# Numerators of two q tiles in one go, and exponentials taken after the transposition

## The chip, the cores and the metric

The kernel runs on one core of a Trainium2 chip. The metric is device time in microseconds (us) of that core. Engines are named as the profile names them: PE (TensorE matmuls) and PEld (its weight loads), DVE (VectorE), ACT (ScalarE), POOL (GpSimd), SP (the queue that issues most DMAs).

## What is computed

The program chains three blocks on 2304 tokens: attention with random features, a two-layer block with softplus, and a gated block. The change touches the attention alone, and in it only the side of the queries. Cut to that:

```
def phi(x):                                   # x is q or k, scaled
    h = einsum('bhsd,md->bhsm', x, omega) - sum(x*x)/2
    h = h - max(h, axis=-1)
    return exp(h) / sqrt(m)
kv  = einsum('bhsm,bhsd->bhmd', k_p, v);  z = sum(k_p, axis=2)
num = einsum('bhsm,bhmd->bhsd', q_p, kv)
den = einsum('bhsm,bhm->bhs', q_p, z) + 1e-06
x   = num / den                               # B=4, H=8, S=576, D=64, m=128
```

For queries a factor that is the same for all 128 features falls out of num/den, so the kernel needs only exp(projection - its maximum).

## The kernel before

The 2304 tokens are cut into 18 q tiles of 128 tokens; each tile has two units of four heads (unit u belongs to tile u // 2, its second unit is odd). A loop over t = 0 to 21, here called turns, works on several tiles at once. Four kinds of PE work stand in a turn, and the text calls them by letters:

- **T** (`q_turn`, L390): eight transpositions of `qp` of tile t-2, two units of four heads; ACT then copies each unit out of PSUM to `qpt` (L392).
- **P** (`q_feat`, `project`, L93 on `qt`): twelve matmuls that project tile t. DVE takes the maximum over the features of each head, negated (`nmax`, L332), and ACT takes the exponential with that maximum as its bias, one instruction of 128x128 for each head (`features`, L337). `QLAG` holds the exponentials of one unit back by one.
- **N** (`q_num`, L93 on `kv,qpt`): numerators and denominators of tile t-3 (`NLAG`), sixteen matmuls of 64 columns for a unit's tile pair (32 instructions in the trace). DVE then adds 1e-6 (`den`, L407), takes the reciprocal (L408) and scales (`xt`, L411, 128x256 a unit).
- **X** (`x_turn`, L420): four transpositions of `xt` of tile t-4 (`XLAG`); ACT copies them to `xs`, and SP writes them to HBM.

So `xt` of a tile is made one turn before its X. Between these stand other steps: `split_q` casts a later q tile on DVE (L285) and subtracts on POOL (L286); `step` pumps a queue of jobs: at first the widening of weights (`Job`, L135 to L188: 128x1024 instructions on ACT and DVE), and from turn 10 on the operands of the next block (`operands`, L445 and L455, 128x768, read back from HBM). In turns 18 to 20 `fill` puts the first matmuls of the next block between. PSUM has eight banks in one pool (`ps`), which all of T, P, N and X share. A scheduler orders each engine's instructions from this program and sets the waits; every engine runs its own list strictly in that order.

Of the kernel before, what the change touches and what calls it, by code (L numbers as in the profile page):

```python
# [19 lines left out]
F32 = mybir.dt.float32  # L20
# [3 lines left out]
AF = mybir.ActivationFunctionType  # L24
ALU = mybir.AluOpType
# [3 lines left out]
M = 128  # L29
# [6 lines left out]
PSUM = bass.MemoryType.PSUM  # L36
DRAM = bass.MemoryType.DRAM
TLAG = 2
NLAG = 3
XLAG = 4  # L40
HALF = 64
PRE = 1
# [2 lines left out]
QLAG = 1  # L45
# [17 lines left out]
FILL = [18, 19, 20]  # L63
URGENT = 300
LINE = 32


@with_exitstack
def body(ctx: ExitStack, tc: tile.TileContext, q, k, k_rest, v, v_rest, om_t, w_in, w_out, w12, w3, wo, out):
    nc = tc.nc  # L70
    cp = ctx.enter_context(tc.tile_pool(name="cp", bufs=1))
    sm = ctx.enter_context(tc.tile_pool(name="sm", bufs=1))
    M_ = ctx.enter_context(tc.tile_pool(name="M_", bufs=14))
# [6 lines left out]
    def ps():  # L80
        return ps_.tile([128, 512], F32, tag="ps", name="ps")
# [156 lines left out]
    def step(rate):  # L238
        due[0] += rate
        while due[0] > 0:  # L240
            if not pump_one():
                due[0] = min(due[0], 2.0)
                break
            due[0] -= 1
# [25 lines left out]
    def pair(name, bufs):  # L270
        n = small.get(name, (None, 1))[1]
        if n:
            small[name] = sm.tile([128, 2, 4], F32, tag=name, bufs=bufs, name=name), 0
        else:
            small[name] = small[name][0], 1
        return small[name][0][:, 1 - bool(n)]
# [4 lines left out]
    def lined(pool, n, **kw):  # L281
        return pool.tile([128, -(-n // LINE) * LINE], F32, **kw)[:, :n]

# [25 lines left out]
    def load_q(t):  # L309
        if t < NT // 128:  # L310
            raw[t] = Q_.tile([128, 512], F32, tag="rawq", bufs=4, name="rawq")
            nc.sync.dma_start(out=raw[t], in_=q[t])

    def split_q(t):
        if t < NT // 128:
            if len(qbuf) < QBUF:
                qbuf.append(Q_.tile([128, 2, 512], FR, name=f"qt{len(qbuf)}"))
            qt = qbuf[t % QBUF]
            split(qt[:, 0, :], qt[:, 1, :], raw[t])
            qts[t] = qt.rearrange("p x (c t) -> p x c t", c=4)  # L320

    def project(lhs):
        pj = ps()
        for p in range(2):
            a = lhs(p)
            if len(a) == 2:
                mm3(pj[:, 256 * p:256 * p + 256], *a, *om_s, True, True)
            else:
                matmul(pj[:, 256 * p:256 * p + 256], *a, om, True, True)
        pj = pj.rearrange("p (h m) -> p h m", h=4)  # L330
        nmax = pair("nmax", 4)
        nc.vector.tensor_reduce(out=nmax, in_=pj, axis=AX.X, op=ALU.max, negate=True)  # L332
        return pj, nmax

    def features(pj, nmax, dst):
        for h in range(4):
            nc.scalar.activation(out=dst[:, h, :], in_=pj[:, h, :], func=AF.Exp, bias=nmax[:, h:h + 1])  # L337

    waiting = []

    def flush(n):
        while len(waiting) > n:
            waiting.pop(0)()
# [14 lines left out]
    def matmul_half(o, a, b, start, stop):  # L358
        for c in range(0, a.shape[-1], HALF):
            matmul(o[c:c + HALF], a[:, c:c + HALF], b, start, stop, skip_group_check=True)  # L360

    def kv_sum(i):
        b, g = divmod(i, 2)
        if g == 0:
            kvs[b] = lined(Q_, H * (D + 1), name=f"kv{b}").rearrange("p (h d) -> p h d", h=H)
        acc = ps()[:, 0:4 * (D + 1)].rearrange("p (h d) -> p h d", h=4)
        for h in range(4):
            for t in range(KT):
                matmul_half(acc[:, h, :], kps[i][:, t, h, :], vt[i][:, t, h, :], h == 0 and t == 0, False)
            r = 2 * (b // 2) + g  # L370
            matmul_half(acc[:, h, :], kpr[r][:, h, :], vrest[:, b % 2, r, h, :], False, h == 3)
        nc.scalar.copy(out=kvs[b][:, 4 * g:4 * g + 4, :], in_=acc)

    qp, qpt, xt = {}, {}, {}

    def q_feat(u):
        t, g = divmod(u, 2)
        p = project(lambda p: [qts[t][:, x, 2 * g + p, :] for x in range(2)])

        def exps():  # L380
            qp[u] = M_.tile([128, 4, M], F32, tag="m", name="qp")
            features(*p, qp[u])

        waiting.append(exps)
        flush(QLAG)

    def q_turn(u):
        tp = ps()
        for h in range(4):
            nc.tensor.transpose(tp[:, 128 * h:128 * h + 128], qp[u][:, h, :], ident)  # L390
        qpt[u] = M_.tile([128, 4, 128], F32, tag="m", name="qpt")
        nc.scalar.copy(out=qpt[u], in_=tp.rearrange("p (h t) -> p h t", h=4))  # L392

    def q_num(u):
        t, g = divmod(u, 2)
        nm = ps()
        nm = nm[:, 0:4 * (D + 1)].rearrange("p (h d) -> p h d", h=4)
        lo, hi = 128 * t, 128 * t + 128
        for h in range(4):
            a = lo  # L400
            while a < hi:
                b = a // S
                e = min(hi, (b + 1) * S)
                matmul_half(nm[a - lo:e - lo, h, :], qpt[u][:, h, a - lo:e - lo], kvs[b][:, 4 * g + h, :], True, True)
                a = e
        den = pair("den", 3)[:, :, None]
        nc.vector.tensor_scalar(out=den, in0=nm[:, :, D:D + 1], scalar1=1e-6 * M, scalar2=None, op0=ALU.add)  # L407
        nc.vector.reciprocal(out=den, in_=den)  # L408
        if g == 0:
            xt[t] = M_.tile([128, H, D], F32, tag="m", name="xt")  # L410
        nc.vector.tensor_tensor(  # L411
            out=xt[t][:, 4 * g:4 * g + 4, :], in0=nm[:, :, 0:D],
            in1=den.to_broadcast([128, 4, D]), op=ALU.mult,
        )

    def x_turn(t):
        tp = ps()
        x = xt[t].rearrange("p h d -> p (h d)")
        for c in range(KD):
            nc.tensor.transpose(tp[:, 128 * c:128 * c + 128], x[:, 128 * c:128 * c + 128], ident)  # L420
        xs = Q_.tile([128, KD, 128], F32, tag="xs", bufs=2, name="xs")
        nc.scalar.copy(out=xs, in_=tp.rearrange("p (c t) -> p c t", c=KD))
        nc.sync.dma_start(out=xd[:, :, 128 * t:128 * t + 128], in_=xs)
# [287 lines left out]
    nt = NT // 128  # L711
    begun = None

    def fill():
        nonlocal begun
        if begun is None:
            until(lambda: 0 in ready and win[0].done)
            x = Up1(0, 0, UP_RATES["Up1"][0])
            begun = x, x.begin_parts()
        next(begun[1], None)  # L720

    for t in range(nt + XLAG):
        for g in range(2):
            if 0 <= t - TLAG < nt:
                q_turn(2 * (t - TLAG) + g)
        for g in range(2):
            if t < nt:
                q_feat(2 * t + g)
            else:
                flush(0)  # L730
            step(JOB_Q[0 in xo])
        if t < nt:
            split_q(t + 2)
            load_q(t + 4)
        if t == 1:
            kv_sum(2 * B - 1)
            kstack.close()
            pools["X0"] = ctx.enter_context(tc.tile_pool(name="X0", bufs=28, side="right", reuse_waits="tile"))
        if 0 <= t - NLAG < nt:
            for g in range(2):  # L740
                q_num(2 * (t - NLAG) + g)
        if t >= XLAG:
            x_turn(t - XLAG)
            for c in range(2):
                if t - XLAG == 2 * N // 128 * (c + 1) - 1:
                    xo[c], ops = operands(c, xd, "X0")
                    queue += ops
        if t in FILL:
            fill()
# [426 lines left out]
```

## Time and profile before

| | us |
|---|---|
| median of 3 runs (815.7 to 816.96) | 816.19 |
| the profiled execution | 816.59 |
| its span, first to last instruction | 814.8 |
| PE busy, share of the span | 804.7 (99%) |
| DVE busy | 594.1 (73%) |
| ACT busy | 443.2 (54%) |
| granted TensorE clock, mean | 0.999 |

The turns with q tiles fill the stretch from about 53 to 137 us of the span; what comes before are the keys, what comes behind are the two dense blocks. A busy share over the whole span hides that stretch: there DVE and ACT are nearly full at times, and PE is the engine with gaps. Times in the rows below are from the start of the span. Where a row merges several instructions ("x8"), its time is that from the start of the first to the end of the last; two instructions of an engine overlap by some 0.08 us, so the distance from start to start is what an instruction takes of its engine.

### The profile page before, as it was taken

To read this page: it belongs to the slowest core of one execution; us is meant where nothing else is said; L and a number is where in the kernel's file an instruction comes from. 1 tells how busy PE (TensorE), PEld (TensorE's weight loads), DVE (VectorE), ACT (ScalarE), POOL (GpSimd) and SP (SyncE) were. 2 spreads that over 40 slices of the span, in tenths; PEclk is the share of its full clock that TensorE was granted. 3 is DMA by queue.
4 is the path that set the end of the run, shared out by engine and by line. 5 is a ranking of instruction groups with operands and counts; after the bars stand their busy time and mean duration, and the time that the engine had idled before them with its cause. 6 is when DMAs were issued, how large, how long until landed. Compare 5 with 4: busy or idle time off the path is not lost.

```text
span 814.8 us, 14545 instructions
## 1 busy us (share of the span) xinstructions
PE 804.7 (99%) x5520; PEld 755.6 (93%) x5520; DVE 594.1 (73%) x1005; ACT 443.2 (54%) x863; POOL 43.7 (5%) x38
## 2 busy tenths in 40 slices
PE   7999999999999999999999999999999999999998
PEld 6998989999999998888888889999999998889998
DVE  4888799878756666754569633898888866888861
ACT  6899998557545665755456422422334223674330
POOL 4623310000000000000000000000000000000000
PEclk9999999999999999999999999999999999999999
DMA  8733535756545457778984632455466556353212
GB/s 283 279 133 89 186 86 164 243 183 225 199 158 192 165 203 243 233 247 303 331 297 152 220 97 83 159 208 176 165 229 217 188 173 233 119 166 124 73 65 77
DMA packets 75717, 150.04 MB, mean 184 GB/s; under 512 B 7168, under 2 KB 44672, under 8 KB 75648
## 3 DMA queue, kind: packets, MB, share of 16 engines
q1 hardware_dynamic: 64560, 101.94, 37.6%
q10 hardware_dynamic: 11088, 47.18, 16.9%
q8 instruction: 43, 0.70, 0.4%
q14 instruction: 26, 0.21, 0.1%
HBM read 98.24 MB, written 50.86 MB: 183 GB/s over the span
## 4 chain that ended last, share of the span: by engine, by line
PE 85%; DVE 5%; ACT 4%; DMA 3%; issue 1%; SPq 0%; DVEq 0%; ACTq 0%
PE ps L93 84%; ACT kp L337 2%; DMA xq<-xd 1%; PE ps L390 1%; DVE s L445 1%; DMA raw<-in_w_in 1%; PE ps L420 1%; DVE nmax L332 1%; DVE xt L411 1%; ACT qp L337 1%; DVE qt L285 0%; DVE c L500 0%; DMA xd<-xs 0%; ACT f L135 0%; ACT raw L136 0%
## 5 line engine op out<-in xcount | busy, mean ns | idle before, releaser
L93 PE MATMUL ps<-dhi,lo 128*128 128x512 f32 (+1 forms) x320 | 117.7, 368 | 0.0
L93 PE MATMUL ps<-dlo,hi 128*128 128x512 f32 (+1 forms) x320 | 117.7, 368 | 0.0
L93 PE MATMUL ps<-dhi,hi 128*128 128x512 f32 (+1 forms) x320 | 117.5, 368 | 0.0
L621 DVE TENSOR_TENSOR dlo<-dn,dhi 128x512 fp32r<-128x512 f32 (+1 forms) x80 | 50.5, 635 | 48.4 <-ACT dhi L620 26.7
L620 ACT CAST dhi<-dn 128x512 fp32r<-128x512 f32 (+1 forms) x80 | 45.6, 576 | 56.9 <-DVE dlo L621 30.3
L500 DVE TENSOR_TENSOR c<-ps,u 128x384 f32<-128x384 f32 x144 | 71.4, 548 | 0.8
L93 PEld LDWEIGHTS ps<-dlo,hi 128*128 128x128 f32 x320 | 60.3, 189 | 10.1
L93 PEld LDWEIGHTS ps<-dhi,lo 128*128 128x128 f32 x320 | 60.3, 189 | 10.1
L93 PEld LDWEIGHTS ps<-dhi,hi 128*128 128x128 f32 x320 | 60.3, 189 | 9.8
L500 DVE TENSOR_TENSOR u<-ps,p 128x384 f32<-128x384 f32 x48 | 26.7, 555 | 58.0 <-PE ps L93 52.5
L135 ACT ACTIVATE f<-raw,bias 128x1024 f32<-128x1024 int16 (+2 forms) x43 | 46.6, 1090 | 33.5 <-DVE lo L176 8.5
L540 ACT ACTIVATE c<-c 128x384 f32<-128x384 f32 x72 | 35.0, 524 | 47.5 <-DVE c L500 47.5
L332 DVE TENSOR_REDUCE nmax<-ps 128x4 f32<-128x512 f32 x72 | 47.6, 680 | 17.8 <-PE ps L93 12.3
L139 DVE SCALAR_TENSOR_TENSOR f<-raw,f 128x1024 int32<-128x1024 f32 (+2 forms) x43 | 45.8, 1066 | 17.8 <-ACT raw L136 17.5
L507 ACT COPY p<-ps 128x384 f32<-128x384 f32 x48 | 22.9, 477 | 61.7 <-PE ps L93 52.6
L136 ACT ACTIVATE raw<-raw,bias 128x1024 f32<-128x1024 int16 (+2 forms) x43 | 46.3, 1082 | 0.4
L145 DVE SCALAR_TENSOR_TENSOR f<-raw,f 128x1024 int32<-128x1024 int32 (+2 forms) x43 | 45.0, 1046 | 0.6
L337 ACT ACTIVATE qp<-ps,nmax 128x128 f32<-128x128 f32 x144 | 42.8, 508 | 0.0
L337 ACT ACTIVATE kp<-ps,nmax 128x128 f32<-128x128 f32 x128 | 35.5, 489 | 8.2 <-DVE nmax L332 8.2
L93 PE MATMUL ps<-xs1h,thi 128*128 128x384 f32 x96 | 32.3, 336 | 0.3 <-DVE c L500 0.3
L93 PE MATMUL ps<-xs2h,thi 128*128 128x384 f32 x96 | 32.3, 336 | 0.0
L93 PE MATMUL ps<-xs2h,tlo 128*128 128x384 f32 x96 | 32.2, 335 | 0.0
(237 smaller groups left out, 2269.6 us busy)
## 6 DMA issues: line engine op xcount, KB each, us to landing
dn<-gd SPq DMA_DIRECT2D x64, 256.0 KB, 3.9
raw<-in_w ACTq DMA_DIRECT2D x16, 1023.8 KB, 5.2
gd<-c SPq DMA_DIRECT2D x80, 192.0 KB, 2.8
pd<-c SPq DMA_DIRECT2D x48, 192.0 KB, 2.5
raw<-in_w_out ACTq DMA_DIRECT2D x10, 767.8 KB, 4.6
raw<-in_w_in ACTq DMA_DIRECT2D x6, 1023.8 KB, 5.1
rawq<-in_q SPq DMA_DIRECT2D x18, 256.0 KB, 2.8
xd<-xs SPq DMA_DIRECT2D x18, 256.0 KB, 3.0
```

Of the source, the lines that this page charges most:

```text
L93: nc.tensor.matmul(out=o, lhsT=a, rhs=b, start=start, stop=stop, **kw)
L135: nc.scalar.activation(out=self.f, in_=top, func=AF.Relu, scale=TOP, bias=bias[:, 0:1])
L136: nc.scalar.activation(out=self.words(1, F32, 2), in_=top, func=AF.Identity, scale=TOP, bias=bias[:, 1:2])
L139: nc.vector.scalar_tensor_tensor(out=self.f.bitcast(I32), in0=self.words(1, F32, 2), scalar=-2.0 ** 31, in1=self.f, op0=ALU.max, op1=ALU.min)
L145: nc.vector.scalar_tensor_tensor(out=fi, in0=self.words(0, I32, 2), scalar=13, in1=fi, op0=ALU.logical_shift_right, op1=ALU.bitwise_or,)
L332: nc.vector.tensor_reduce(out=nmax, in_=pj, axis=AX.X, op=ALU.max, negate=True)
L337: nc.scalar.activation(out=dst[:, h, :], in_=pj[:, h, :], func=AF.Exp, bias=nmax[:, h:h + 1])
L500: nc.vector.tensor_tensor(out=z, in0=bank, in1=y, op=ALU.add)
L507: nc.scalar.copy(out=p6, in_=b1)
L540: nc.scalar.activation(out=dst, in_=src, func=AF.Softplus)
L620: nc.scalar.copy(out=hi, in_=got[m])
L621: nc.vector.tensor_tensor(out=lo, in0=got.pop(m), in1=hi.bitcast(F32), op=ALU.subtract)
```

## The change

`NLAG` goes. The numerators now run in even turns alone, for tiles t-4 and t-3 together, four units at once, straight ahead of X of tile t-4. And for the second unit of tiles 0 to 9 (`TURNED`) the order of exponential and transposition is swapped: DVE adds the negated maximum to the projection (`qs`, 128x512, PSUM to SBUF), PE transposes that, and ACT takes the exponential as it leaves PSUM, one instruction of 128x512 where the copy was. The four exponentials of 128x128 of that unit fall away. Ten units are treated so.

```
+TURNED = range(10)
     def q_feat(u):
...
-        waiting.append(exps)
-        flush(QLAG)
+        if turned_first(u):
+            qp[u] = M_.tile([128, 4, M], F32, tag="m", name="qs")
+            nc.vector.tensor_tensor(out=qp[u], in0=p[0], in1=p[1][:, :, None].to_broadcast([128, 4, M]), op=ALU.add)
+            flush(0)
+        else:
+            waiting.append(exps)
+            flush(QLAG)
     def q_turn(u):
...
-        nc.scalar.copy(out=qpt[u], in_=tp.rearrange("p (h t) -> p h t", h=4))
+        tp = tp.rearrange("p (h t) -> p h t", h=4)
+        if turned_first(u):
+            nc.scalar.activation(out=qpt[u], in_=tp, func=AF.Exp)
+        else:
+            nc.scalar.copy(out=qpt[u], in_=tp)
...
-        if 0 <= t - NLAG < nt:
-            for g in range(2):
-                q_num(2 * (t - NLAG) + g)
+        if t % 2 == 0 and 0 <= t - XLAG < nt:
+            for u in range(2 * (t - XLAG), 2 * (t - XLAG) + 4):
+                q_num(u)
```

Three places show what the scheduler makes of it. The lines of the changed kernel stand twelve further down (L407 is L419, L411 is L423, and so on); L389 is the new add. The first place is DVE in turns 2 to 4 (`tlo` and `lo` are weight jobs).

DVE before, ahead of and at the first `xt`:

```order
L332 TENSOR_REDUCE nmax<-ps 128x4
L188 TENSOR_TENSOR tlo<-t,thi 128x1024
L407 TENSOR_SCALAR den<-ps 128x4 x2
L408 RECIPROCAL den<-den 128x4 x2
L411 TENSOR_TENSOR xt<-ps,den 128x256 x2
```

DVE now, from the same `tlo` to the first `xt`:

```order
L188 TENSOR_TENSOR tlo<-t,thi 128x1024
L389 TENSOR_TENSOR qs<-ps,nmax 128x512
L332 TENSOR_REDUCE nmax<-ps 128x4
L176 TENSOR_TENSOR lo<-f,hi 128x256
L176 TENSOR_TENSOR lo<-f,hi 128x512
L332 TENSOR_REDUCE nmax<-ps 128x4
L285 CAST qt_893<-rawq 128x512
L389 TENSOR_TENSOR qs<-ps,nmax 128x512
L419 TENSOR_SCALAR den<-ps 128x4 x2
L420 RECIPROCAL den<-den 128x4
L419 TENSOR_SCALAR den<-ps 128x4
L423 TENSOR_TENSOR xt<-ps,den 128x256
```

Between that `tlo` and the first `xt` there now stand two adds, two reductions, two `lo` and a cast; three more adds stand farther ahead.

The second is PE from the end of one P (`omh`, `oml` are the two halves of omega, `qt_893` a q tile's buffer) to the T behind it. PE before, in turn 6:

```order
L93 MATMUL ps<-omh,qt_893 128x256 x2
L93 MATMUL ps<-oml,qt_893 128x256
L93 MATMUL ps<-omh,qt_893 128x256
L93 MATMUL ps<-kv_304,qpt 64x65 x16
L420 MATMUL ps<-ident,xt 128x128 x4
L390 MATMUL ps<-ident,qp 128x128 x8
```

PE now, in turn 6:

```order
L93 MATMUL ps<-omh,qt_893 128x256
L93 MATMUL ps<-kv_304,qpt 64x65 x32
L432 MATMUL ps<-ident,xt 128x128 x2
L398 MATMUL ps<-ident,qp 128x128 x4
L432 MATMUL ps<-ident,xt 128x128 x2
L398 MATMUL ps<-ident,qs 128x128 x4
```

N is twice as long, X follows it at once and takes `xt` of that same N, and T stands between the halves of X and behind them.

The third is DVE in turns 11 and 12, where the jobs are operands of the next block (`s` and `xa11l`). DVE before, in turn 11:

```order
L332 TENSOR_REDUCE nmax<-ps 128x4
L445 TENSOR_TENSOR s_1824<-xq 128x768
L407 TENSOR_SCALAR den<-ps 128x4 x2
L408 RECIPROCAL den<-den 128x4
L455 TENSOR_TENSOR xa11l<-xq,xa11h 128x768
L411 TENSOR_TENSOR xt<-ps,den 128x256
```

DVE now, from turn 11 up to the first `xt` of turn 12:

```order
L332 TENSOR_REDUCE nmax<-ps 128x4
L457 TENSOR_TENSOR s_1794<-xq 128x768
L467 TENSOR_TENSOR xa11l<-xq,xa11h 128x768
L332 TENSOR_REDUCE nmax<-ps 128x4 x2
L457 TENSOR_TENSOR s_1853<-xq 128x768
L419 TENSOR_SCALAR den<-ps 128x4 x2
L420 RECIPROCAL den<-den 128x4
L419 TENSOR_SCALAR den<-ps 128x4
L423 TENSOR_TENSOR xt<-ps,den 128x256
```

The work in front of `xt` has not become more over two turns, but X now comes right behind the N that feeds it.

## Rows read from the trace of the kernel before

**Rows 1.** Busy time by engine in five stretches; busy us and instructions (x), clock, DMA.

```profile
59.09:72.04 12.95, 11.77 (x141) 10.37 (x137) 12.85 (x24) 12.95 (x42) 2.67 (x3) 1.00 0.23 66
72.04:96.15 24.11, 24.03 (x339) 22.63 (x338) 18.30 (x61) 22.62 (x70) 8.95 (x7) 1.00 0.44 132
96.15:121.36 25.21, 25.02 (x339) 22.80 (x338) 23.37 (x55) 24.74 (x72) 5.13 (x4) 1.00 0.44 138
121.36:136.95 15.59, 15.55 (x206) 13.98 (x205) 14.15 (x41) 13.34 (x31) 0.00 (x0) 1.00 0.63 187
136.95:814.00 677.05, 674.11 (x3647) 635.13 (x3645) 481.34 (x761) 320.75 (x493) 0.00 (x0) 1.00 0.55 186
```

The columns behind the length are PE, PEld, DVE, ACT, POOL, granted clock, DMA share and GB/s.

**Rows 2.** Timeline of PE around the first X: start, us, engine, line, what.

```profile
69.67 1.15 PE L93 MATMUL ps<-kv,qpt 128*64 128x65 f32 x32 [0.83 <-DVE xt L411]
70.75 0.65 PE L420 MATMUL ps<-ident,xt 128*128 128x128 f32 x4
...
72.04 0.36 PE L93 MATMUL ps<-omh,qt 128*128 128x256 f32 x1
```

**Rows 3.** Timeline of DVE in the same turns, up to the weight job behind `xt`.

```profile
58.38 1.89 DVE L139 SCALAR_TENSOR_TENSOR f<-raw,f 128x1024 int32<-128x1024 f32 x1 [0.60 <-ACT raw L136]
60.31 1.23 DVE L145 SCALAR_TENSOR_TENSOR f<-raw,f 128x1024 int32<-128x1024 int32 x1
...
65.13 1.16 DVE L285 CAST qt<-rawq 128x512 fp32r<-128x512 f32 x1
...
66.81 1.97 DVE L188 TENSOR_TENSOR tlo<-t,thi 128x1024 fp32r<-128x1024 f32 x1
...
69.10 0.75 DVE L411 TENSOR_TENSOR xt<-ps,den 128x256 f32<-128x256 f32 x2
...
70.97 1.01 DVE L176 TENSOR_TENSOR lo<-f,hi 128x256 fp32r<-128x256 f32 x2
```

**Rows 4.** Timeline of POOL: two of its subtractions.

```profile
66.42 1.28 POOL L286 TENSOR_TENSOR qt<-rawq,qt 128x512 fp32r<-128x512 f32 x1 [0.42 <-DVE qt L285]
...
108.93 1.29 POOL L286 TENSOR_TENSOR qt<-rawq,qt 128x512 fp32r<-128x512 f32 x1 [9.30 <-DVE den L407]
```

**Rows 5.** Timeline of PE in a steady turn: P, N, X, T and the next P.

```profile
80.28 0.36 PE L93 MATMUL ps<-omh,qt 128*128 128x256 f32 x1
...
81.87 1.15 PE L93 MATMUL ps<-kv,qpt 128*64 128x65 f32 x32
82.96 0.66 PE L420 MATMUL ps<-ident,xt 128*128 128x128 f32 x4
83.45 1.04 PE L390 MATMUL ps<-ident,qp 128*128 128x128 f32 x8
84.24 0.36 PE L93 MATMUL ps<-omh,qt 128*128 128x256 f32 x1
```

**Rows 6.** Timeline of DVE in that turn.

```profile
81.27 0.69 DVE L332 TENSOR_REDUCE nmax<-ps 128x4 f32<-128x512 f32 x1 [1.06 <-PE ps L93]
81.92 0.43 DVE L285 CAST qt<-rawq 128x512 fp32r<-128x512 f32 x1
82.26 0.68 DVE L332 TENSOR_REDUCE nmax<-ps 128x4 f32<-128x512 f32 x1
82.86 0.37 DVE L407 TENSOR_SCALAR den<-ps 128x4 f32<-128x4 f32 x2
...
83.42 0.76 DVE L411 TENSOR_TENSOR xt<-ps,den 128x256 f32<-128x256 f32 x2
```

**Rows 7.** Timeline of ACT in that turn: copies of X and T, exponentials.

```profile
84.17 1.08 ACT L392 COPY qpt<-ps 128x512 f32<-128x512 f32 x2
85.13 2.20 ACT L337 ACTIVATE qp<-ps,nmax 128x128 f32<-128x128 f32 x8
```

**Rows 8.** Timeline of DVE, later: a cast beside POOL, and a job of 128x768.

```profile
109.00 1.50 DVE L285 CAST qt<-rawq 128x512 fp32r<-128x512 f32 x1
...
137.42 0.94 DVE L455 TENSOR_TENSOR xs2l<-s,xs2h 128x768 fp32r<-128x768 f32 x1
```

More of the change, by code (lines that the diff above doesn't have):

```diff
@@ L38 @@
 TLAG = 2
-NLAG = 3
 XLAG = 4
@@ L374, in body, with turned_first @@
     qp, qpt, xt = {}, {}, {}
+    def turned_first(u):
+        return u % 2 == 1 and u // 2 in TURNED
     def q_feat(u):
```

## The prediction

> **What bounds the kernel now.** I read first the busy time of every engine in stretches [rows 1]. From 136.95 to the end PE is busy 674.11 of 677.05 us, so whatever the q turns lose or win ahead of that passes to the end one to one; nothing behind it can take up a delay. In the q turns PE is not everywhere full. In the first stretch 12.95 - 11.77 = 1.18 us of PE is idle, while ACT (12.95 of 12.95) and DVE (12.85) are packed. The second and the third hold the same 339 instructions of PE, six turns each, but take 24.11 and 25.21 us. DVE there has 18.30 and 23.37 us of work, ACT 22.62 and 24.74.
>
> Next the timeline of PE around the first X [rows 2]. N of tile 1 stood 0.83 us for an `xt` on DVE (N needs the bank that this `xt` reads); X begins at 70.75, the next P at 72.04. What DVE did until then [rows 3]: it waited 0.60 for ACT once (58.38), and otherwise worked without a pause. Three of its instructions are longer than they need be: L139 1.89 us where L145 of the same size takes 1.23; the cast at 65.13 1.16; `tlo` at 66.81 1.97. Each begins just after a subtraction on POOL: the one at 66.42 lasts 1.28 [rows 4], and `tlo` comes 0.39 behind its start.
>
> Last a steady turn. Its length is 84.24 - 80.28 = 3.96 us [rows 5]: P 1.59, N 1.09, X 0.49, T 0.79, with no gap. DVE waits 1.06 us for PE in that turn [rows 6], and a cast takes 0.43. ACT needs 2.20 us for eight exponentials and 1.08 for the two copies of T [rows 7]. So in steady turns PE is the bound. Six times 3.96 are 23.76, so the second stretch holds 0.35 us of stalls and the third 1.45, though PE counts as busy in them (a matmul that waits behind its start is drawn longer).
>
> **The change part by part.** All sums are against the profiled execution's own 816.59; the median of the runs is 816.19, 0.40 lower, and the last step goes to that scale.
>
> *ACT.* Per treated unit four exponentials go, half of 2.20, say 1.0 after overlap, and an exponential of the copy's size takes the copy's place; the nearest row is that copy, 0.5. ACT so loses 1.0 of work ten times. On a path that goes PE, DVE, PE this earns nothing by itself.
>
> *DVE.* Ten adds of 128x512 out of PSUM come. Not in the trace; the nearest rows are the reduction of 128x512 out of PSUM, 82.86 - 82.26 = 0.60 [rows 6], and two `xt` of 128x256 out of PSUM in 0.76, or 0.68 for 512 columns. I take 0.60. In a steady turn they fit into the idle 1.06; ahead of the first `xt` DVE has no such idle time.
>
> *Term A, up to the end of the first X.* The first `xt` began at 69.10 [rows 3]. Ahead of it stand now in addition: five adds, 3.00; two reductions, 1.20; two `lo`, 0.93 (70.97 to the next instruction). That is 5.13. What may go: the 0.60 wait for ACT, since ACT is lighter; and the three lengthenings, L139 1.89 - 1.23 = 0.66, the cast 1.16 - 0.43 = 0.73, `tlo` some 0.9 (1.97 against the 1.0 to 1.2 of such instructions), because the casts which release POOL stand elsewhere in DVE's list. Together 2.89. As POOL's subtractions are as many as before, I put one lengthening of 0.7 back. The first `xt` then begins at 69.10 + 5.13 - 2.89 + 0.70 = 72.04, and X 0.42 + 0.13 later (its own length, and the step to PE), 72.6 in place of 70.75: **+1.8**. Bounds: no lengthening stays, +1.1; L139's and `tlo`'s stay too, +3.4.
>
> The lengthening again, by itself: beside a subtraction that began at 108.93 [rows 4] a cast took 1.50 us at 109.00 [rows 8], and 0.43 alone. [...]
>
> *Term B, three pairs of turns, up to 96.15 before.* PE's work per pair is the same: 2 x 1.59 + 2.18 + 2 x 0.49 + 2 x 0.79, or 7.92. But X follows the N that feeds it. Count from the start of P in the turn with N. The second reduction starts at 82.26 - 80.28 = 1.98 and takes 0.60; then an add, 0.60; two `den` and a reciprocal, 0.14 each (0.56 for four, 82.86 to 83.42); `xt` 0.42 and 0.13 to PE. That is 4.15 at the latest, some 4.05 where a `den` goes ahead. PE is through with N at 1.59 + 2.18 = 3.77. So X waits about 0.3, three times, 0.9; the 0.35 of stalls before go. **+0.6**; bounds -0.3 (all waits hidden) and +1.5 (a cast or a lengthening in the way each time, 0.3 more).
>
> *Term C, six turns, up to 121.36 before.* No adds any more, but jobs of 128x768 on DVE, 0.94 [rows 8], or 0.87 from start to start. One stands straight ahead of the `den` and `xt` of turn 12. Working as in B with the job for the add: 1.98 + 0.60 + 0.87 + 0.42 + 0.55 = 4.42, a wait of 0.65; with a lengthening by POOL like the cast's at 109.00, 1.5. Turn 14 likewise, 0.5 to 1.6; turn 16 0 to 0.15. The middle is 2.3, and the 1.45 of before goes. **+0.9**; bounds -0.3 and +1.8.
>
> *Term D, the last turns, 121.36 to 136.95.* PE was full, 15.55 of 15.59. X stands behind its N twice more, with DVE at 14.15 of 15.59 [rows 1]: one job's 0.87, once half of it. The first matmuls of the next block stand between and hide a third or so. **+0.8**; bounds -0.2 (all hidden) and +1.3.
>
> *Nothing:* SP's writes of `xs` keep their number and move by at most one turn; the next block begins on PE behind the turns in any case. The N of four units takes four banks at once, but P and T have passed by then.
>
> Sum: 1.8 + 0.6 + 0.9 + 0.8 = 4.1; 816.59 + 4.1 = 820.7, **820.3** on the median's scale. The bounds' sums are +0.3 and +8.0; as the four are apart from one another, I keep about 3 to either side: 817.0 to 823.4.
>
> **The rivals.**
>
> *R1, faster: ACT was what held the turns.* For it: ACT has no idle time in the first stretch and half a microsecond in the third [rows 1], and just there PE loses time, while in the second, where ACT has 1.5 us free, PE loses little. ACT's relief of some 1.0 per unit lets banks of PSUM go earlier. If it carries, the 1.18 and the 1.45 go and A to D bring no wait: 816.59 - 2.63 = 814.0, 813.6 on the median's scale. It decides if the first X starts ahead of 70.75. Against it: the wait ahead of the first X is DVE's [rows 2], and DVE gets 5.1 us more ahead of it.
>
> *R2, no change.* The adds vanish in DVE's idle time as in a steady turn [rows 6], ACT's relief takes the stalls of the first and the third stretch, and the waits of X behind N cost what that gives. It needs A below about 1.5, and C at its lower bound: 816.2, give or take 1.2. For it: 1.06 us of idle DVE in a steady turn holds one add of 0.60 in either turn of a pair. Against it: DVE is packed in the first stretch, and X is the one step that the change has moved next to its source.
>
> That the change doesn't do what it says I leave out: the maximum is one number for each token and head, and may be added ahead of the transposition.
>
> **How the numbers follow.** The forecast gets 0.64, R1 0.20, R2 0.16. About 0.2% (1.6 us) is what a measurement of this kernel can tell from no change: faster is below 814.6, slower above 817.8. R1 lies nearly all below 814.6; a small part of the forecast's lower end lies between. So faster 0.19, same 0.19, slower 0.62. The range goes from 813.5, which keeps half of R1, to 823.4; I leave out some 0.1 at either end.
>
> **What would show it.** A: the first `xt` starts near 72.0 and the first X near 72.6; ahead of 70.75 speaks for R1, and if DVE's adds take 0.68 rather than 0.60, A is 0.4 larger. B: in turns with N of four units PE shows a wait of about 0.3 for `xt`, in the others none, pairs of about 8.2. C: two waits of 0.7 to 1.5 behind jobs. D: two more, of less than 0.9. Behind the turns PE's work should be unchanged at about 677 us. The forecast falls if X finds its `xt` ready, and above all if stalls go that I count as PE's own time: a pair of steady turns below 7.92.

## The result, and the profile after

The changed kernel takes 825.31 us (median of five runs, 823.26 to 826.7) against 816.96 for the kernel before (now of five runs; 816.19 was the median of three): a measured ratio of 1.0098, with a 95% interval of 1.0085 to 1.011. Its profiled execution takes 825.02, with a span of 823.2. So it is slower, as forecast, but by 8 us and not by 4, and 1.9 us beyond the upper end of the range; 0.8 of these are the kernel before, which came out that much higher.

The windows of the profile after, cut where [rows 1] were cut by the work on PE (first T of that stretch, P of tile 5, P of tile 11, P of tile 17, last X); columns as there:

```profile
59.21:74.64 15.43, 11.52 (x139) 10.83 (x137) 15.03 (x34) 10.78 (x29) 5.61 (x4) 0.96 0.17 54
74.64:99.66 25.02, 24.07 (x339) 23.30 (x337) 20.02 (x59) 15.48 (x43) 8.39 (x7) 0.96 0.45 131
99.66:128.09 28.43, 23.29 (x339) 22.42 (x337) 24.06 (x61) 25.50 (x73) 6.00 (x4) 1.00 0.40 121
128.09:144.51 16.42, 13.69 (x200) 12.88 (x199) 14.00 (x37) 13.59 (x30) 0.00 (x0) 1.00 0.51 159
144.51:822.00 677.49, 674.90 (x3652) 636.10 (x3650) 479.48 (x759) 320.15 (x492) 0.00 (x0) 1.00 0.55 186
```

The same 339 instructions of PE took 24.11 and 25.21 us before and take 25.02 and 28.43 now. PE, which had 1.2 and 0.2 us without work in the first and the third stretch, has 3.9 and 5.1 there. ACT has become lighter in the first two (10.78 of 15.43, 15.48 of 25.02), and nothing came of it. In two stretches the granted clock is not 1.00. Behind the last X the rest takes what it took before (677.49): what the q turns lose arrives at the end.

The timeline of PE around the first X, after (to be read beside [rows 2]):

```profile
67.92 2.22 PE L93 MATMUL ps<-kv,qpt 128*64 128x65 f32 x64
72.79 0.41 PE L432 MATMUL ps<-ident,xt 128*128 128x128 f32 x2 [2.65 <-DVE den L419]
...
74.64 0.56 PE L93 MATMUL ps<-omh,qt 128*128 128x256 f32 x1
```

And of DVE and POOL in those turns, after (beside [rows 3, 4]): L139, `tlo`, an add, the first `xt`; then two subtractions of POOL.

```profile
58.72 1.23 DVE L139 SCALAR_TENSOR_TENSOR f<-raw,f 128x1024 int32<-128x1024 f32 x1 [0.56 <-ACT raw L136]
...
67.03 1.21 DVE L188 TENSOR_TENSOR tlo<-t,thi 128x1024 fp32r<-128x1024 f32 x1
...
71.23 0.68 DVE L389 TENSOR_TENSOR qs<-ps,nmax 128x512 f32<-128x512 f32 x1
...
72.22 0.42 DVE L423 TENSOR_TENSOR xt<-ps,den 128x256 f32<-128x256 f32 x1
```

```profile
67.24 2.14 POOL L286 TENSOR_TENSOR qt<-rawq,qt 128x512 fp32r<-128x512 f32 x1 [3.48 <-DVE qt L285]
71.44 1.26 POOL L286 TENSOR_TENSOR qt<-rawq,qt 128x512 fp32r<-128x512 f32 x1 [2.06 <-DVE qt L285]
```

N ends at some 70.1, and PE stands 2.65 us until DVE has come to the first `xt` at 72.22. `tlo` takes 1.21 now, and POOL's subtraction, which began 0.21 behind it, 2.14: the two have changed roles against [rows 3, 4]. The add at 71.23, beside the subtraction at 71.44, lengthened neither: 0.68 and 1.26, where an add at 59.86 took 0.68 and a subtraction at 74.05 took 1.27.

Here is what the prediction had no term for. The window from that X to the next X, in the profile after:

```profile
72.79:77.14 4.35, 4.35 (x25) 4.35 (x26) 2.15 (x7) 1.67 (x3) 1.27 (x1) 0.61 0.39 120
```

The granted clock is 0.61 in it, and 0.50 from 73.50 to 76.50; a matmul of P takes 0.21 there from start to start, and 0.12 in the next P. At the full clock the same piece takes 2.77 (shown below), so 1.58 us went there.

Four windows of pairs and single turns, after: a pair with a wait of X (0.48), the next pair, whose tile 10 has no add, and the turns 12 and 14.

```profile
86.52:94.70 8.18, 7.70 (x116) 7.46 (x114) 6.88 (x20) 5.22 (x16) 2.58 (x3) 1.00 0.49 130
94.70:102.39 7.69, 7.69 (x115) 7.41 (x114) 6.11 (x19) 6.38 (x21) 2.55 (x3) 1.00 0.61 187
102.39:110.48 8.09, 5.20 (x91) 4.81 (x90) 6.08 (x17) 5.83 (x16) 0.76 (x1) 1.00 0.59 188
113.23:119.77 6.54, 4.95 (x91) 4.71 (x90) 6.54 (x19) 5.88 (x17) 4.72 (x3) 1.00 0.16 47
```

A pair without a wait takes 7.69; before it took 2 x 3.96 = 7.92. A turn with N of four units takes 4.96 without a wait (94.70 to 99.66), so turn 12 stands 3.1 us and turn 14 1.6. What stood in turn 12, first on DVE, then ACT, then PE:

```profile
104.40 0.96 DVE L457 TENSOR_TENSOR s<-xq 128x768 f32<-128x768 f32 x1 [2.06 <-DMA xq<-xd]
105.32 0.96 DVE L467 TENSOR_TENSOR xa11l<-xq,xa11h 128x768 fp32r<-128x768 f32 x1
...
107.39 0.95 DVE L457 TENSOR_TENSOR s<-xq 128x768 f32<-128x768 f32 x1
...
108.66 0.42 DVE L423 TENSOR_TENSOR xt<-ps,den 128x256 f32<-128x256 f32 x1
```

```profile
104.45 0.83 ACT L464 CAST xa11h<-xq 128x768 fp32r<-128x768 f32 x1 [1.96 <-DMA xq<-xd]
105.19 0.36 ACT L337 ACTIVATE qp<-ps,nmax 128x128 f32<-128x128 f32 x1
```

```profile
105.61 1.65 PE L93 MATMUL ps<-kv,qpt 128*64 128x65 f32 x48 [0.92 <-ACT qp L337]
109.23 0.41 PE L432 MATMUL ps<-ident,xt 128*128 128x128 f32 x2 [1.97 <-DVE den L419]
```

DVE and ACT wait 2 us for `xq`, the read-back of X from HBM for the next block. On DVE two jobs, two reductions and the third job stand between it and `xt`; on ACT one last exponential waits behind the cast of `xq`, and N waits for it. The chain of waits of the kernel before runs through the read-back, too, from the `xs` of tile 5:

```profile
91.65 0.59 ACT xs L422
...
92.26 2.84 DMA xd<-xs
...
95.19 4.46 DMA xq<-xd
...
99.67 0.96 DVE s L445
```

The first of its two reads landed 0.46 us ahead of P of tile 12 (100.13), and the wait of DVE for it, 0.84, was nearly hidden: the turns 12 and 13 took 8.06, what two turns without a stall and 0.14 make. The stalls of that stretch stood behind them:

```profile
100.13:108.19 8.06, 8.06 (x116) 7.49 (x113) 8.06 (x21) 8.06 (x23) 0.00 (x0) 1.00 0.57 184
108.19:116.91 8.72, 8.56 (x115) 7.63 (x114) 8.72 (x26) 8.72 (x28) 2.67 (x3) 1.00 0.22 64
```

Now it lands 2.01 behind P of tile 12 (104.40 and 102.39). SP's queue, after, shows where that arose:

```profile
95.48 0.33 SPq L312 DMA_DIRECT2D rawq<-in_q  x1
95.90 0.53 SPq L435 DMA_DIRECT2D xd<-xs  x1
98.22 0.33 SPq L312 DMA_DIRECT2D rawq<-in_q  x1
98.86 1.20 SPq L450 DMA_DIRECT2D xq<-xd  x2
```

From X of tile 5 (93.47 on PE) to its write, 2.43 us pass in place of 1.35, since a q tile's load stands ahead of the write on SP and is not issued until 95.48 (`xs` was ready at 94.74): 1.08. The read takes 5.5 in place of 4.46: 1.06. The last q load was issued just ahead of it (98.22), which the kernel before issued behind it (97.17, the read at 95.19); whether that is what lengthens it the experiments leave open. And X of tile 5 is 0.3 nearer to P of tile 12. That is 2.4, against 2.01 + 0.46.

### The profile page after: what moved, and what is told of

The parts are those of the page before. It is cut to its first block, busy times and chain, and to the rows that moved or that the text cites. A ratio compares the mean times of both kernels' runs of the same rounds, so it can differ in the third digit from the quotient of the medians.

```text
span 823.2 us, 14521 instructions
## 1 busy us (share of the span) xinstructions
PE 801.9 (97%) x5520; PEld 756.4 (92%) x5520; DVE 597.0 (73%) x1015; ACT 433.9 (53%) x823; POOL 45.8 (6%) x38
## 4 chain that ended last, share of the span: by engine, by line
PE 79%; DVE 1%; issue 0%; ACT 0%; DVEq 0%; ACTq 0%
PE ps L93 79%; DVE c L512 0%; DVE f L145 0%; DVE s L993 0%; DVE u L512 0%; DVE wt L916 0%; ACT xs3h L1005 0%; DVE lo L176 0%; DVE c L1062 0%; ACT th L928 0%; DVE xs3l L1009 0%; DVE t L152 0%; DVE xa12l L1009 0%; DVE xs1l L1009 0%; DVEq L512 0%
## 5 line engine op out<-in xcount | busy, mean ns | idle before, releaser
L139 DVE SCALAR_TENSOR_TENSOR f<-raw,f 128x1024 int32<-128x1024 f32 (+2 forms) x43 | 45.1, 1050 | 20.1 <-ACT raw L136 20.1
L93 PE MATMUL ps<-xa11h,lo 128*128 128x384 f32 x96 | 32.2, 335 | 0.0
L93 PE MATMUL ps<-xs3h,thi 128*128 128x384 f32 x96 | 32.2, 335 | 0.0
```

Of the source, the lines that this page charges most:

```text
L93: nc.tensor.matmul(out=o, lhsT=a, rhs=b, start=start, stop=stop, **kw)
L139: nc.vector.scalar_tensor_tensor(out=self.f.bitcast(I32), in0=self.words(1, F32, 2), scalar=-2.0 ** 31, in1=self.f, op0=ALU.max, op1=ALU.min)
```

## The experiments

Each is an edit of the changed kernel, but for f1 and g1, which are that kernel again, and g3, an edit of the kernel before. For the traces, this table gives what every kernel lost against the kernel before in four stretches of its profiled execution, from the starts of P of tiles 0, 5, 11, 17 and of the last X on PE (before: 53.56, 72.04, 96.15, 121.36, 136.47). They answer to the terms A to D; x is the measured ratio of its runs to those of the kernel before that ran with them, and not the plain quotient of the medians.

```
                          A      B      C      D      sum    x
changed kernel          +2.49  +0.91  +3.22  +1.31  +7.93  1.0098
e1 pairs only           +2.81  -0.90  +4.50  +1.05  +7.46  1.0093
e2 adds only            -0.20  -0.11  +1.39  +0.88  +1.96  1.0044
e3 GAP 6                +2.38  -0.13  +3.64  +0.03  +5.92  1.0137
e4 X in odd turns       +0.58  -0.95  +0.49  +0.04  +0.16  1.0004
e5 read-back earlier    +2.15  +2.83  +1.64  +0.04  +6.66  1.0081
e6 PE kept busy         +2.41  -0.09  +3.12  +1.33  +6.77  1.0099
e7 X odd, no adds       +1.52  -1.22  +1.22  +0.05  +1.57  1.0046
e8 X odd, adds 3 to 13  +1.36  -1.19  +0.42  +0.32  +0.91  1.0049
f1 changed, again       +3.12  +0.69  +5.40  +1.38 +10.59  1.0111
f2 five buffers         +2.55  +0.85  +2.46  +1.56  +7.42  1.0117
f3 e2, five buffers     -0.03  -0.14  +1.63  +0.09  +1.55  1.0005
f4 e4, five buffers     +0.30  -0.96  +1.30  +0.07  +0.71  1.0005
g1 changed, again       +2.38  -0.06  +5.16  +1.04  +8.52  1.0109
g2 e6, again            +2.60  -0.08  +4.89  +1.07  +8.48  1.0086
g3 before, five buffers +0.07  -0.03  -0.01  -0.01  +0.02  0.9998
g4 adds only, again     -0.16  -0.14  +1.78  +0.85  +2.33  1.0024
```

The sum and x need not agree. The sum leaves out where the q turns begin (52.9 to 55.1) and what follows the last X (677.8 to 680.0 us), which scatter by some 2 us over the traces, and it is one execution: e4's trace is of its slowest run of ten (819.61), e3's of its fastest of five (823.03).

**Which half of the change costs.** Two kernels with one half each.

```
-TURNED = range(10)
+TURNED = range(0)
```

> The numerators in pairs as changed, but no unit treated (no add on DVE, all exponentials ahead of the transposition). Theory 1 (the loss comes from X standing straight behind the N that feeds it, and from the operands' read-back in turn 12; the adds only make the first X later and so lower the clock): the first X comes at about 70.5 to 71.5 in place of 72.8, no half clock behind it, the waits in turns 12 to 20 stay: 819.5 to 822. Rival (the ten adds on DVE are the loss, the pairing costs nothing): 816 to 817.5, no waits of X over 0.3.

It took 823.82 against 816.5: ratio 1.0093 (1.0078 to 1.0108), beyond what theory 1 gave it, and clear of the rival. The pairing alone costs nearly all. The first X did not come earlier without the adds but later, at 74.14 (0.44 of that a later start of the q turns). What PE waited for between 50 and 160 us, total, times, longest:

```profile
PE ps L432 <- DVE den L419: 6.7, 5, 2.0
PE ps L93 <- ACT qp L337: 2.2, 1, 2.2
PE ps L398 <- ACT qp L337: 1.8, 3, 1.1
PE ps L432 <- ACT qp L337: 1.7, 1, 1.7
```

Without the adds it is exponentials on ACT that T waits for ahead of the first N, and the X waits of 0.47 in turns 6 and 8 are gone (B is -0.90). So the adds cost some 0.8 us there (B is -0.09 in e6, whose clock did not fall, and -0.90 without adds), and save 0.3 to 0.4 in A.

```
+NLAG = 3
...
-        if t % 2 == 0 and 0 <= t - XLAG < nt:
-            for u in range(2 * (t - XLAG), 2 * (t - XLAG) + 4):
-                q_num(u)
+        if 0 <= t - NLAG < nt:
+            for g in range(2):
+                q_num(2 * (t - NLAG) + g)
```

> The other half: ten units take the add and the exponential behind the transposition, but the numerators stay one tile a turn, one turn ahead of X. Theory 1: X finds its xt ready; only the first N waits a little longer for a bank that xt frees, and turn 12 has the wait for the read-back as before: 815 to 818. Rival (the adds are the loss): 822 to 826.

820.23, ratio 1.0044 (1.0028 to 1.006): between the two, so a miss for theory 1 as well. In the trace the adds win 0.3 where they stand (A and B) and lose in C and D, where there are none. The chain of waits shows the read-back held by SP once more, the last q load (95.56) ahead of it:

```profile
95.56 0.33 SPq L313
...
96.00 5.28 DMA xq<-xd
...
101.30 0.96 DVE s L458
```

The same kernel once more, beside g3 below, gave less:

> The ten adds alone with four buffers, once more, beside g3. If the loss of 3.7 us was real and the buffer mends it: 1.003 to 1.006 of the kernel before. If it was that chip's scatter: within 1.002.

818.83, 1.0024 (1.0013 to 1.0034). The adds alone lose 2 to 4 us.

**X behind its N, or a turn later.** X of both tiles in the odd turn:

```
-        if t >= XLAG:
-            x_turn(t - XLAG)
+        for x in (t - XLAG - 1, t - XLAG) if t > XLAG and t % 2 else ():
+            x_turn(x)
...
-                if t - XLAG == 2 * N // 128 * (c + 1) - 1:
+                if x == 2 * N // 128 * (c + 1) - 1:
```

> The changed kernel with X of both tiles in the odd turn, one turn behind their N. Theory 1: the waits of X for xt (10.5 us in eight places) nearly all go, with them the half clock behind the first; the read-back's wait stays in part (1 to 2 us); a pair of turns takes 7.7: 814 to 817.5. Rival (DVE's work in these turns is the bound, wherever X stands): the wait moves to N or T, 821 or more.

816.6, ratio 1.0004 (0.9994 to 1.0015): the whole loss is gone, with N still of four units, the ten adds, and the same work. Three pairs of turns, in its windows:

```profile
76.95:100.12 23.17, 23.17 (x339) 22.35 (x338) 21.22 (x61) 17.51 (x50) 9.93 (x8) 1.00 0.63 182
```

23.17 for what took 24.11 before: 0.9 us better. It gives this back early, where T waits 1.2 for an add and the next P 0.9, and in turns 12 to 16 with the read-back. That one is late here too, DVE waits 1.77 us for `xq`; but the turns 12 and 13 take 8.96 in place of the changed kernel's 10.84. So a late read-back costs much only where X stands behind the jobs that wait for it. What the adds are worth with X in the odd turn:

```
-TURNED = range(10)
+TURNED = range(0)
```

> X of both tiles in the odd turn, and no unit treated. Tells what the adds bring when X does not stand behind its N. If ACT holds the early turns (as the pairing alone showed, where T and X stood for exponentials): 818 to 820, T waits for exponentials by some 2 us in turns 2 to 4. If the adds bring nothing: 816.6 as with them, within 0.8.

819.61, ratio 1.0046 (1.0027 to 1.0064): with X out of the way the adds bring 3.4 us by the ratios, 1.4 by the traces, two thirds of it in A, where T waits for exponentials without them (1.8 us in three places). Other tiles for the adds, X still in the odd turn:

```
-TURNED = range(10)
+TURNED = range(3, 14)
```

> X in the odd turn; treated are the second units of tiles 3 to 13 in place of 0 to 9, so that DVE has no add in turns 0 to 2, where T stood 1.2 us for one, and ACT is relieved in turns 10 to 13, where both are full. Theory 1: 814.5 to 816. Rival (the exponentials in turns 0 to 2 take as long on ACT as the adds on DVE, and in 10 to 13 the bound only moves from ACT to DVE): 816.5 to 818.

820.35, ratio 1.0049 (1.0034 to 1.0064), against theory 1: T waits for exponentials in the first turns again (1.13 and 0.35), A is 0.8 more than e4's, and the relief of turns 10 to 13 does not show in C beyond e4's. Its A to D lose 0.9 us; the rest of what its trace lost is a start of the q turns 1.6 us later and 1.2 more behind the last X, and the cause of both is open.

**The read-back.** First an edit that was to give it more time:

```
-GAP = 3
+GAP = 6
```

> The changed kernel with three more empty places between the loads of the next block's operands and their first use (GAP 3 to 6). Theory 1 (in turn 12 DVE and ACT stood for the read-back that had not landed, 2.1 us, and everything behind them with it): the wait of DVE for xq goes, turn 12 falls from 8.1 to 5.5 or 6.5 us; some of it comes back as jobs ahead of xt in later turns: 822 to 824.5. Rival (the jobs themselves stand in the way, and the read-back is hidden in that): turn 12 shorter, but turns 14 to 18 longer by as much, 825 within 0.7.

827.26, ratio 1.0137 (1.012 to 1.0154): worse, neither theory's number, but in part by the clock (below): its trace is of the one run at a granted clock of 1.000, 823.03, and the four at 0.994 to 0.998 took 827.3 to 828.7. The scheduler left the first job that reads `xq` where it was (102.86, DVE still waits 2.42 for the read), and put the next one straight ahead of the first `xt`, beside a subtraction of POOL (104.88, 1.27), where it took 1.55:

```profile
102.86 0.96 DVE L457 TENSOR_TENSOR s<-xq 128x768 f32<-128x768 f32 x1 [2.42 <-DMA xq<-xd]
...
105.42 1.55 DVE L457 TENSOR_TENSOR s<-xq 128x768 f32<-128x768 f32 x1
```

So it tells nothing of the read-back: X waited 3.55 here in place of 1.97, N no longer for ACT (0.92 before), and turn 12 took 8.49. Next a read that needs no write later than that of tile 4 (part of the operands are then of the wrong tokens):

```
-                nc.sync.dma_start(out=r, in_=src[:, 2 * kk:2 * kk + 2, 2 * N * c:2 * N * (c + 1)])
+                late_cols = 128 if src is xd and c < 2 else 0
+                if late_cols:
+                    for h in range(2):
+                        at = 2 * N * c + N * h - late_cols * h
+                        nc.sync.dma_start(out=r[:, :, N * h:N * h + N], in_=src[:, 2 * kk:2 * kk + 2, at:at + N])
...
```

> The changed kernel, but the read-back for the next block takes its second half of tokens one tile earlier (so the first two thirds of the operands are of the wrong tokens) and therefore needs no write later than that of tile 4 or 10; the loads are so issued a turn earlier, and the order of the jobs follows them. Theory 1: DVE's wait for xq (2.1 us) and ACT's go, turn 12 falls from 8.1 to some 5.5 to 6.5 us, the total by 1.5 to 3: 822 to 823.8. Rival (DVE and ACT are full there anyway, the wait only stands where the work would): turn 12 falls and turns 10, 14 and 16 take it up, 825 within 0.8.

823.56, ratio 1.0081 (1.0066 to 1.0096), as theory 1 had it in sum, but the table tells more: C falls from 3.22 to 1.64, D to nothing, and B rises by 1.9, since the jobs now stand a turn earlier, between the halves of `xt`, and X waits there:

```profile
96.04 0.44 PE L432 MATMUL ps<-ident,xt 128*128 128x128 f32 x2 [1.20 <-DVE xt L423]
```

Cleaner is a fifth buffer for the q loads, which leaves the lists of PE and DVE word for word and reorders SP: no q load stands between the last write and the read any more.

```
-            raw[t] = Q_.tile([128, 512], F32, tag="rawq", bufs=4, name="rawq")
+            raw[t] = Q_.tile([128, 512], F32, tag="rawq", bufs=5, name="rawq")
```

> The changed kernel with five buffers in place of four for the q tiles' loads. The lists of PE and DVE stay word for word; on SP the last load of a q tile now stands ahead of the last write of X that the read-back needs, not behind it, and no load waits for a buffer ahead of a write. Theory 1 (the read-back lands late because SP held the write of tile 5 for 1.2 us behind a q load, and 4.72 us of turn 12's 8.1 hang on it): xq lands 1 to 1.7 us earlier in its turn, turn 12 shortens by as much, 822.5 to 824. Rival (the read-back is late by its own length of 5.5 us, SP's order does nothing): as the changed kernel within 0.7.

SP's queue, DVE's wait and the window of turn 12 in this kernel:

```profile
96.02 0.53 SPq L435 DMA_DIRECT2D xd<-xs  x1
99.02 1.19 SPq L450 DMA_DIRECT2D xq<-xd  x2
```

```profile
103.58 0.96 DVE L457 TENSOR_TENSOR s<-xq 128x768 f32<-128x768 f32 x1 [1.16 <-DMA xq<-xd]
```

```profile
102.48:109.83 7.35, 5.17 (x91) 4.79 (x90) 6.18 (x17) 5.98 (x16) 0.76 (x1) 1.00 0.59 195
```

The read takes 4.5 us in place of 5.5, DVE's wait falls from 2.06 to 1.16, and turn 12 from 8.09 to 7.35. With the same lists on DVE there are four more traces: waits of 1.96, 2.47, 2.71 and 2.74 go with turns of 8.00 (e6), 8.53 (g2), 9.09 (f1, 0.7 of it at half clock) and 8.81 us (g1). So with these lists turn 12 is longer by 0.9 us for each microsecond that DVE waits for the read-back: that is shown. The write was not issued earlier, as I had expected: a q load still stands ahead of it. In the total nothing showed: 825.79, ratio 1.0117 (1.0097 to 1.0136), beside f1:

> The changed kernel once more, beside the three that follow. Both theories: 1.0098 of the kernel before, 824 to 825.5.

827.42, ratio 1.0111 (1.0094 to 1.0129). The runs of f2 spread over 824.8 to 830.1 and those of f1 over 823.8 to 828.4, too far to show the 0.7 us of turn 12. The same buffer for the adds alone, for X in the odd turn, and for the kernel before:

> The ten adds alone, numerators one tile a turn, with five buffers for the q loads. Theory 1 (what the adds alone lost, 3.7 us, came of the last q load that SP issues ahead of the read-back, where the kernel before issues it behind): the wait for xq falls from 1.77 to under 1 us and 1 to 2 us come back: 818 to 819.5. Rival (the adds' loss is in the order of the jobs on DVE): 820 within 0.8.

> X in the odd turn with five buffers for the q loads: the version that could beat both. Theory 1: the read-back is issued about 1 us earlier, turns 12 to 16 shorten by 0.7 to 1.5: 815 to 816. Rival: 816.6 within 0.6.

> The kernel before with five buffers for the q loads; only SP's list differs, the last q load goes ahead of the read-back in it. If the fifth buffer helps any kernel: 814.5 to 816 against 816.5 to 817.4. If it only mends what the adds lost: the same within 0.7.

They gave 818.22, ratio 1.0005 (0.9995 to 1.0015); 817.76, 1.0005 (0.9996 to 1.0014); and 816.75, 0.9998 (0.9988 to 1.0007). For the kernel before the buffer does nothing. With the adds alone a loss no longer shows (the interval still overlaps that of g4), but not in the way I gave: the wait for `xq` is 2.26 in its trace, not under 1, C stays, and D, the last turns, is what goes (0.88 to 0.09). The order of the jobs on DVE differs as well. Why the adds alone lose is left open. So is what lengthens the read: it took 4.46 to 4.54 us in the kernel before, f2 and g3, and 5.2 to 6.7 in nine traces with a q load issued up to 1.3 us ahead of it, but 4.56 in e8 with a load 0.5 us ahead, and 5.94 in f3 with none nearer than 3.6. No version beats the kernel before.

**The clock.** Twenty transpositions that nobody reads, behind the first N:

```
                 q_num(u)
+            if t == XLAG:
+                tp = ps()
+                for g in range(5):
+                    for h in range(4):
+                        nc.tensor.transpose(tp[:, 128 * h:128 * h + 128], qpt[3][:, h, :], ident)
```

> The changed kernel with twenty more transpositions of 128x128 (about 2.2 us, into a bank that nobody reads) behind the first N, where PE waited 2.65 us for the first X. Theory 1 (the half clock of the 4.4 us behind this X comes of that idle time and cost 1.5 us): X comes at the same time, X, T and P behind it run at the full clock, 1.3 to 1.7 us less: 823 to 824.2. Rival (the clock falls for the idle time ahead of it as a whole, the waits at 64 to 66 included, or not for idleness at all): no gain, 825 within 0.8.

The timeline of PE, and the window from X to X:

```profile
70.01 2.40 PE L758 MATMUL ps<-ident,qpt 128*128 128x128 f32 x20
72.73 0.41 PE L432 MATMUL ps<-ident,xt 128*128 128x128 f32 x2 [0.32 <-DVE den L419]
```

```profile
72.73:75.49 2.76, 2.76 (x24) 2.76 (x25) 1.97 (x7) 1.57 (x3) 1.30 (x1) 1.00 0.27 98
```

X comes when it came, and the piece behind it takes 2.76 in place of 4.35. But the median was 825.0, ratio 1.0099, no gain, and three of its four runs were at a clock of 1.000 (823.5, 825.6, 825.9); the changed kernel was not beside it. Then f1 ran, and its trace has two such pieces, the second behind the waits of turn 12 (1.58 and 1.97):

```profile
73.49:77.84 4.35, 4.35 (x24) 4.35 (x25) 2.09 (x7) 1.67 (x3) 1.28 (x1) 0.61 0.43 115
110.56:115.32 4.76, 4.76 (x29) 4.76 (x30) 2.93 (x9) 4.04 (x11) 0.00 (x0) 0.64 0.20 59
```

Its six runs line up by the mean granted clock: 823.8 at 1.000, 825.3 at 0.998, 827.1 at 0.997, 827.8 to 828.4 at 0.996. That called for the two side by side:

> The changed kernel beside g2. Runs without a half clock about 823.5, with one stretch of it 825, with two 827 to 828.

> The changed kernel with twenty transpositions of 128x128 for nobody behind the first N (the lists of DVE, ACT and SP are those of the changed kernel). Theory 1 (each half-clock stretch costs some 1.6 us and the first follows the 2.65 us in which PE stood): one stretch fewer in nearly every run, 1.2 to 2 us less than g1 in the median. Rival (what g1's slow runs lose comes from elsewhere): the same within 0.8.

g1 took 826.04, ratio 1.0109 (1.0095 to 1.0123), every run at 0.995 to 0.998, and a miss: the three runs at 0.995 and 0.996 took 825.8 to 826.5 and not 827 to 828. g2 823.93, 1.0086 (1.0069 to 1.0104), three of six runs at 1.000 (823.7 to 824.0). That is 2.1 us less by the medians, inside theory 1's expectation but for 0.1; the two intervals still overlap. Clearer is how often the clock stayed full: in 6 of 10 runs of the two kernels with the transpositions, in 1 of 15 of the changed kernel (first runs, f1, g1). So the wait has a part in lowering the clock. But the clock does not order the times of all runs, as e6 and g1 show; the traces also differ in the read-back's wait and outside the q turns. In g1's trace the first X went without a half clock, and turn 12 did not:

```profile
73.64:76.41 2.77, 2.77 (x24) 2.77 (x25) 1.97 (x7) 1.58 (x3) 1.29 (x1) 1.00 0.30 98
109.19:113.94 4.75, 4.75 (x28) 4.75 (x29) 3.19 (x9) 4.23 (x12) 0.00 (x0) 0.64 0.20 59
```

The wait ahead of the first X is 2.65 us in six of the traces (the changed kernel, e3, e5, f1, f2, g1); the clock fell behind it in four (0.61 in the windows of the changed kernel, f1 and f2, 0.67 and then 0.50 in those of e5) and was 1.00 in e3 and g1. In turn 12, with the wait of N for ACT and that of X for DVE (1.9 to 2.0), it fell in the three traces where the first was 1.3 to 1.6 (f1, g1, g2) and in none of the four where it was 0.3 to 0.9 or 2.2 (f2, e6, the changed kernel, e1). Kept busy, PE had no half clock behind the first X in either trace (1.00 in e6 and in g2). Why it fell behind the same wait in four traces and not in the other two is not shown.

## Why the prediction was right and wrong

The sign, the mechanism (X behind the N that feeds it, DVE between them) and the places of the waits were right. The size was not: 4.1 us forecast, 7.9 in the trace. The step that failed is term C, which left out the wait for the read-back, and a term for the clock is missing. All four terms came out above their forecast, so narrowing the bounds' sum of +8.0 to 3 us either side did not hold either.

*Term A.* The first `xt` was put at 72.04 and began at 72.22, the first X at 72.6 and began at 72.79; an add takes 0.60 from start to start; the three lengthenings went, but for 0.5 on one instruction (L155, 0.91 for 0.42), where 0.7 was put back. So the working holds but for one step: the 0.60 wait for ACT was to go and stayed, 0.56 (58.72), and that DVE's other instructions came out some 0.5 shorter than assumed is luck. P of tile 5 came 2.6 later, not 1.8, since PE ran X and T at a granted clock of 0.67 (72.79 to 74.64). As a cause the adds were misjudged: without them (e1) the first X is later still, by ACT. R1 was right on that point, that ACT holds the early turns; it was wrong that relieving ACT would do: with the adds and no pairing A is only 0.2 better (e2, g4), and with the pairing X waits for DVE.

*Term B.* Waits of 0.47, 0.48 and 0 against three of 0.3, and pairs of 8.18 against "about 8.2": the pairs with a wait were right. But it was named as a way to fall that a pair takes less than 7.92, and it does, 7.69 without a wait. An odd turn goes from P to X without the step to N (0.12 in place of 0.21 us), and N of four units ends in 2.05 in place of 2 x 1.09. This gives back 0.23 a pair. Without the 1.0 of half clock in P of tile 5, B is -0.1 (e6 and g1 have -0.09 and -0.06) for +0.6 forecast: that it came out at +0.9 is luck.

*Term C, the step that failed.* Forecast +0.9, at most +1.8; it is +3.2. Turn 14 waits 1.6 (0.5 to 1.6 forecast) and turn 16 0.6 (at most 0.15), but turn 12 3.1 where 0.65 to 1.5 were allowed. By the 0.9 above, 1.9 of these are the 2.06 of the read-back, and what is left, 1.2, is as forecast. The prediction disposed of SP in one sentence under *Nothing*: the writes of `xs` "keep their number and move by at most one turn". It did not follow the write to its reader, though the chain of waits of the kernel before runs through it. The 0.84 us for which DVE waited for `xq` there could be seen, but little hung on it (8.06 for two turns) as long as X took an `xt` of the turn before.

*Term D.* Waits of 1.79 and 0.94 for 0.87 and half of it; +1.31, at the bound. Three jobs stand ahead of `xt` there and not one, and DVE waits for the next read-back too, 0.80 ahead of the first wait and 0.57 ahead of the second:

```profile
131.29 0.96 DVE L457 TENSOR_TENSOR s<-xq 128x768 f32<-128x768 f32 x1 [0.80 <-DMA xq<-xd]
```

*The clock.* Not a word in the prediction. Each piece at half clock costs 1.6 to 2 us where it stands, and the traces of the changed kernel have one or two of them. The miss of 3.8 us in the trace is C's 2.3, D's 0.5, the clock's 1.6 (in A and B) and A's 0.1, less the 0.7 by which B itself came out lower.

*The rivals.* R1 decided at 70.75; X came at 72.79. R2 needed A below 1.5. Both fell where they said. What R2 described, adds that vanish in DVE's idle time, is nearly what e4 shows: with X a turn later the change costs nothing, and brings nothing.

## What to carry to other kernels

Two steps that feed each other want a turn between them; putting them side by side to save a switch (0.23 us a pair here) exposes the slower engine's whole queue. When a step moves, follow what it writes to the one that reads it, through the DMA queue and the loads that share it, and count from landing to first use. And where a change opens a wait on PE of 2 us, add to the wait the work behind it that may run at half the clock (1.6 us here, behind a wait of 2.65), and give the range room for it, since it does not come in every run (in four of six traces here).

## What the runs showed of the hardware

That behind waits of 1.3 to 2.7 us a PE that is busy otherwise went to half its clock for some 3 to 4 us was not expected: 0.61 of the full clock over 4.35 us in the changed kernel's trace, and a fall in four of six traces with the very same wait, 2.65, while behind a longer one of 3.55 us (e3) the clock was 1.00. With twenty transpositions in the wait the clock behind it was 1.00 in both traces. The same read of 768 KB, the first of the read-back's two, took between 4.46 and 6.7 us from issue to landing. A subtraction of POOL took 2.14 in place of 1.27 when DVE's `tlo` had begun 0.21 us earlier.
